# A fourth piece of w_in gets its low part on VectorE, and the written-out order and engine choices are replaced

## The chip, the cores and the metric

The kernel runs on one core of a Trainium2 chip. The metric is device time in microseconds (us). The core has five engines with queues of their own: TensorE (PE; PEld is its weight load), VectorE (DVE), ScalarE (ACT), GpSimd (POOL) and SyncE (SP), which only issues transfers here. Nearly all transfers are issued on SP's queue, in its order.

## The reference

Attention (4 batches, 8 heads, 576 tokens, 64 per head) with rotary tables, then a layer that multiplies by w_in (512 x 2048), applies a leaky function with a slope of its own per column, and multiplies by w_out; then a soft mixture of 8 experts with 4 slots each.

```python
x1, x2 = (x[..., :half], x[..., half:])            # rotate, for q and k
q_rot = concatenate([x1 * cos - x2 * sin, x1 * sin + x2 * cos])
attn = softmax(q_rot @ k_rot.T / sqrt(64));  x = (attn @ v) as 2304 x 512
h = x @ w_in
g = np.maximum(h, 0.0) + alpha * np.minimum(h, 0.0)
x = g @ w_out
logits = x @ phi                                   # 2304 x 32
d = softmax over tokens;  slot_input = d.T @ x     # 32 x 512
slot_out[e] = np.maximum(slot_input[e] @ w1[e], 0.0) @ w2[e]
out = softmax over slots of logits @ slot_out
```

## The kernel before

**Attention.** Heads go in pairs p = 0 to 3. Rotated keys and queries are made by `prep_qk` (loads, two multiplications by the tables, a sum; the first pair of batch 0 by `first_qk`, L341 and L346, in four parts so that the first scores come early). TensorE makes scores (L483 in batch 0; L492 to L496 in the later ones), VectorE their maximum (L501), ScalarE the exponential (L506), ScalarE or GpSimd the scaling (L228, L232). Batch 0 turns the probabilities on TensorE (L581, L631), copied out at L222 or L224; the other batches turn them in 32 x 32 blocks on VectorE (L568) and through DRAM. Products with the values are 20 matmuls (L665) for 256 tokens of a pair, or for the 64 that are left.

**First layer.** Tokens go in 9 blocks of 256. A chunk is 128 columns of w_in for one block: 12 matmuls of 128 x 256 in float16 (L842), 16 chunks to a block. Both operands are pairs of float16, a high part and a low part (what the high part leaves), and a chunk multiplies high by high, high by low and low by high. `logit` (L884) adds each group of four chunks to the block's logits. "Slots" of a block (`slots_late`, L1036) is a burst of 128 small matmuls, and stands eight times; the last block has another form (L1000).

**Weights.** w_in comes as 64-bit floats in 8 pieces j of 256 columns (`prep_w`, L704). For each: a load of 1 MB (L714), three VectorE instructions that build 32-bit floats (L736, L738, L740), the bound by ScalarE (L748), TensorE's spread of it over the partitions (L248) with a short VectorE chain, then the high part. The low part is made in one of two ways: for j below 5 by `split`, in two halves: a scaled diagonal (on one of three engines), TensorE multiplies it with the 32-bit weights (L288) and subtracts the high part (L289), and ScalarE or VectorE copies the result out. For j of 5 and more it is one VectorE instruction:

```python
nc.vector.scalar_tensor_tensor(dst(1), xv(), sw[:, j:j + 1], dst(0), ALU.mult, ALU.subtract)
```

The chunks of piece j wait for its low part (`w_ops[0, j]`). Pieces of w_out transposed come after, and give the weights of the logits (`wphi`).

**Order.** Every operation is listed in a Plan with its engine, what it depends on and the buffers it uses. Where an operation may go to one of several engines, `choose` takes the next digit of the string ENGINES. The string ORDER holds a permutation of all operations; they are issued in it, and each engine and queue works through its own ones in that sequence. `order` asserts that each stands behind what it needs. The costs and due times in the `op` calls take no part in the order that is run. In the tail, loads of w_out and of the expert weights (L1194, L1249) wait until attention's buffers are free, and some until the last block's slots are done.

Of the kernel before, what the change touches and what calls it, by code (L numbers as in the profile page):

```python
# [32 lines left out]


ENGINES = (
    "020000000201020000001001101011101110101010000110000100202000100200021000112000100110020010020000002011102020000200010001"
    "000000000020000200000202001000000000001202000200010000000000201010000100001002011000002202000000020120010000000000202000"
    "012211020020001000002020000000010000200220000021000000002000002002202200120220021000200202000202002200200220200021000202"
    "222000210110000000201020120000102220000002000201000201221000000200022000202001202200000220000000002200000000001102000021"
    "220000000000202000202000000201000220000000002200000202002000200001200000000200220000212010012010000201000000000000000100"  # L40
    "000101001001001010100001011100000011001001012010110000000000000110100100000100001111000000000000001000110100101100110001"
    "00010000000000101000101010000001000000011011001011000100000110011011010101"
)


ORDER = (
    "c-m!F2UrzH*WNRG@1<P23Mh(5FM<?B3?hjUeg%8^qsDw1#eywZ5aahL7-K=KNo+CZx1eZ5VnGnasDX%-"
    "2%<E_f=IDMka7{YyYtV??nQh)c<%1Z*>m3Wo^xjA%$<OIzB3>f0rD@vTQB7yq;44eM5BgrM|)0u@YwHeqhDu{|6|9;`au4It`2~Fe{e{5d8lvzha(X;23NeY0#mzU(<amG0A+<9Xu@ux"
    "e$VZ04H!g>93f?B-"
    "q3b^==})pdpW*d28WGj94_Crqt5J|A2erpJ5?6>I4Y`Nxb%EH7zzdu7uiFsN9>J)^T(p<&9Cm9x<K>D*4p@%jX6MNn{S@duEXxR<qsjvJUBe`zGvi9Yg6cY*Y9p%&C@ZjlZW>%^=&Wpc"  # L50
    ">CTXW_i2gl|jWra)ZhW7N;Y3^($u$#DxHaK-"
    "r7F&W+GRXi{}P^J(h!lD95t9Ch8%r7?2pJ0}qD1e@IkcerW!+F^GDn7B39^tH_ndaHtbGmZMi(XYdAyH<Ncs(Its%OXGA^r5+4rEO6UF!p<^e)X!w0p3HS(6<K(q|leIt1|-"
    "w%eI0s&{70;7KTu%{A2Du2!B3W^T@eKT^IbwD`Pa2fC)4NLeAA*&;DIuTkTRR4F8M2IyES2!yQu)&wUMEBzLL(4V<#xnOU!x3xR8<JC_cvICADrwQX<64ag11n+!!hQ203XTBu3Y`jy~"
    "xZDR7Azu-"
    "IZ8o-f=V_M~8<3HnWJR30o*W+#nKN(a2OWSXH+GKpHe_-)}5m%?BFE~6KQ~>JIv!Uj2e$x4vhc1IM;28)@_Gd%Kv_3zmj>DN5)@au%-_)d2uyV|mpOTYo4BJA{wiq+`*1Py-TE_7GYew"
    "hPPlpba{mu+h#wE{;-Vv0zf0N$HStnK7vo~zo0723G*iQ!9)Z;@d_QVC=T^D85*4U>lMU8TnkI3G;b)84)a%(VNe)<dd^36WV5NOz6J|%Bxh;O7_sDZ(m+wp7Bm4E{-"
    "k(zZEr#MucNB6wP?>;!oxPG%<`u`}dw62>zNIyJnTqh4M3E=>3cY`2x99+76HdoJZ!ll%f^=|$_Bes+tEQFCK`<&ipv3hFTNXT_AhuE@5>QM$0c|5n?IJ;r0GW&%)l)2Xg9jhwM-"
    "?QSu^@EYU@28$WGQg&X-"
    "%*=dwB`5v4;Gfzo{wL<#iZE;9hiYmn@k;hc6{Xc$#{Fi#h>4C;lQCaJ_Z)(#TV#w*yixJW@)DmnDZw?b3R#oz!dTA^#k4;&6qtxsog&_%Xh$$hz_s&`mPT_s0>Rtin{x-"
    "w&y=t|NDMl!Kab+R;Cp#Zt5E2)XAcH+v4`YWj`)9X@okrqMZ1uA{aaKKTjQuiXEDVpforRNE=t#&pXT34kA|WhGTQa9k*CfF~MMB<i4-^w1UylJn(+tivSizxbso9HsRy=M5oHU-"  # L60
    "G8L+Ub*K4%p+^|R>fEO!9S0C6r7fDCnHP*zrwWe1n?Z4Wb*8A{A24WLCyEhP1A>zjT?~v;q&)eGyC)zyJ=LwnWW6W5)C({0`#c>FrE@!Zv*Qg%gEQD<9LCw|HZ`Q%*oTd`5TK`UMl;a@"
# [103 lines left out]
def attn_moe_softmoe(ctx, tc, qx, kx, vx, w_in, w_out, alpha, phi, w1, w2, tab, msks, w_out_t, out):  # L165
# [538 lines left out]
    def prep_w(j, which, due):  # L704
        c = {}
# [53 lines left out]
        u = [s_raw, s_wx, s_w]  # L759
        o = run["raw"] = op(DMA, 2913, due + WD, load, [run["raw"]], takes=[s_raw], uses=[s_raw])  # L760
# [365 lines left out]
    n = 0  # L1126
# [21 lines left out]
    for b in range(B):  # L1148
        r = 64 * (b % 2)
# [33 lines left out]
    wo, s_wo, wo_op = {}, {}, {}  # L1183
# [39 lines left out]
    for base, half in [(b, h) for b in range(0, 24, 4) for h in range(2)] + [(b, h) for h in range(2) for b in (24, 28)]:  # L1223
        if True:
            for i in range(base, base + 4):
# [5 lines left out]
                n = 2 if key[:3] == (1, 1, 1) else 1  # L1231
# [443 lines left out]
```

## Time and profile before

| | us |
|---|---|
| median of 3 runs (564.83 to 568.68) | 564.88 |
| profiled execution | 566.71 |
| its span | 564.8 |
| TensorE busy in the span | 529.4 |
| VectorE busy | 478.4 |
| ScalarE busy | 335.7 |
| GpSimd busy | 269.5 |

The span is what the profile's times count from, and lies 1.9 us under the time of the execution that it was taken in. Busy time counts compute instructions only. A busy share is an average over stages with different limits, so the stages are read one at a time. In a table by stage a line gives the stretch, its length, then for PE, PEld, DVE, ACT and POOL in turn the busy us (and instructions), then the granted TensorE clock, the DMA share and GB/s. In a timeline the first two numbers are the start and the time from first start to last end of the instructions merged in that line.

### The profile page before, as it was taken

The numbers are of one execution on the slowest core, as the hardware profiler recorded it, in microseconds if no ns is written. First come the engines' busy times: TensorE is split into PE (matmuls) and PEld (weight loads), VectorE is DVE, ScalarE is ACT, GpSimd is POOL, SyncE is SP. The second block draws the span as 40 slices with busy tenths as digits, with TensorE's granted clock in tenths as the row PEclk, the third lists the DMA queues.
The fourth block names the chain that finished last, engine by engine and source line by source line (L and its number), as shares of the span: only waits on it lengthen the run. The fifth ranks groups of instructions, "written<-read, shape, count | busy, mean of one in ns | idle before, by whom it ended". The sixth has DMA issues, their size and how long they took to land.

```text
span 564.8 us, 14752 instructions
## 1 busy us (share of the span) xinstructions
PE 529.4 (94%) x5752; PEld 392.9 (70%) x5752; DVE 478.4 (85%) x1085; ACT 335.7 (59%) x817; POOL 269.5 (48%) x254
## 2 busy tenths in 40 slices
PE   3799999999999899999989899999999999999994
PEld 1455655778787587787867688877678877864464
DVE  4999999999999599999989599999866899865363
ACT  2999999898787377576677358576421222330220
POOL 3676854598879833678773478854110000001000
PEclk9999999999999899999999899999999999999998
DMA  8995758447999878698997778987864998899998
GB/s 296 395 339 181 233 172 243 136 145 264 291 327 332 272 234 298 199 344 296 324 288 231 260 233 279 335 283 247 268 230 166 412 408 332 324 379 381 404 366 238
DMA packets 80805, 160.74 MB, mean 285 GB/s; under 512 B 5344, under 2 KB 44640, under 8 KB 80736
## 3 DMA queue, kind: packets, MB, share of 16 engines
q1 hardware_dynamic: 80320, 159.45, 81.8%
q8 instruction: 45, 0.74, 0.5%
q10 hardware_dynamic: 416, 0.36, 0.3%
q14 instruction: 24, 0.20, 0.1%
HBM read 115.75 MB, written 36.96 MB: 270 GB/s over the span
## 4 chain that ended last, share of the span: by engine, by line
PE 73%; DVE 11%; ACT 6%; DMA 6%; issue 3%; SPq 1%; POOL 0%; DVEq 0%; ACTq 0%; POOLq 0%
PE ph L842 32%; PE pv L665 12%; PE st L496 8%; DMA xw<-in_moe_w_dram 4%; PE pu L1036 4%; PE lg L884 3%; DVE mm L501 2%; ACT e L506 2%; PE st L483 2%; DMA vt<-in_v_dram 1%; DVE w L740 1%; PE st L492 1%; DVE w L738 1%; PE pt L581 1%; PE st L494 1%
## 5 line engine op out<-in xcount | busy, mean ns | idle before, releaser
L842 PE MATMUL ph<-xt,w 128*128 128x256 f16 x1536 | 183.9, 273 | 2.1 <-issue 1.6
L842 PEld LDWEIGHTS <-w 128*128 128x128 f16 x1728 | 162.0, 98 | 31.8 <-issue 9.2
L506 ACT ACTIVATE e<-st,mm 128x576 f32<-128x576 f32 x144 | 106.2, 739 | 44.2 <-DVE mm L501 40.0
L501 DVE TENSOR_REDUCE mm<-st 128x1 f32<-128x576 f32 x144 | 105.3, 739 | 10.8 <-PE st L496 8.0
L232 POOL TENSOR_SCALAR e<-e,mm 128x576 f32<-128x576 f32 (+1 forms) x76 | 59.2, 785 | 86.6 <-DVE mm L532 56.1
L853 ACT ACTIVATE rl<-ph 128x256 f32<-128x256 f32 x110 | 41.1, 380 | 83.8 <-PE ph L842 79.6
L375 POOL TENSOR_TENSOR xn<-xn,tabs 128x576 f32<-128x576 f32 x52 | 78.7, 1522 | 25.4 <-DMA xn<-in_k_dram 12.5
L665 PE MATMUL pv<-ET,vt 128*64 128x256 f32 (+1 forms) x640 | 80.2, 397 | 1.1 <-ACT e L506 0.9
L568 DVE STREAM_TRANSPOSE tb<-e 128x512 f32<-128x512 f32 (+1 forms) x108 | 75.3, 705 | 0.5 <-ACT e L228 0.4
L496 PE MATMUL st<-ks,qs 128*128 128x288 f32 x384 | 74.3, 316 | 1.1 <-issue 0.9
L860 DVE SCALAR_TENSOR_TENSOR g<-rl,oma,ph 128x256 f32<-128x256 f32 x144 | 66.2, 465 | 9.6 <-ACT rl L853 8.6
L665 PEld LDWEIGHTS pv<-ET,vt 128*64 128x64 f32 (+1 forms) x640 | 44.5, 140 | 29.9 <-issue 6.0
L228 ACT ACTIVATE e<-e,mm 128x576 f32<-128x576 f32 (+1 forms) x78 | 56.6, 736 | 7.5 <-DVE mm L532 7.1
L496 PEld LDWEIGHTS st<-ks,qs 128*128 128x128 f32 x384 | 54.5, 189 | 5.7 <-issue 3.0
L876 DVE STREAM_TRANSPOSE gb<-g 128x512 f32<-128x512 f32 x64 | 43.7, 692 | 0.2
L483 PE MATMUL st<-ks 64*128 64x288 f32 (+1 forms) x168 | 30.2, 453 | 10.2 <-DVE ks L346 8.0
L378 POOL TENSOR_TENSOR xn<-xn 128x576 f32<-128x576 f32 x23 | 34.2, 1491 | 1.3
L400 POOL TENSOR_TENSOR qs<-xn,qs 64x576 fp32r<-64x576 f32 x21 | 30.8, 1466 | 7.9 <-ACT qs L222 4.7
L1056 POOL MEMSET edt<- 128x256 f32 x1 | 0.3, 312 | 68.5 <-DVE lp L1025 68.5
L483 PEld LDWEIGHTS st<-ks 64*128 64x128 f32 (+1 forms) x168 | 17.1, 191 | 20.2 <-POOL ks L346 7.4
L506 ACT ACTIVATION_READ_ACCUMULATOR e<-st,mm 128x1 f32 x144 | 28.4, 197 | 0.0
L228 ACT ACTIVATE xt<-pv,vb 128x256 f16<-128x256 f32 x26 | 12.2, 471 | 22.3 <-PE pv L665 19.7
(201 smaller groups left out, 820.7 us busy)
## 6 DMA issues: line engine op xcount, KB each, us to landing
sc<-tb SPq DMA_DIRECT2D x48, 576.0 KB, 4.2
ET<-sc SPq DMA_DIRECT2D x24, 1152.0 KB, 7.6
xw<-in_moe_w_dram SPq DMA_DIRECT2D x42, 512.0 KB, 9.0
xn<-in_k_dram SPq DMA_DIRECT2D x15, 576.0 KB, 6.4
xn<-in_q_dram SPq DMA_DIRECT2D x15, 576.0 KB, 5.6
wraw<-in_moe_w_in_dram SPq DMA_DIRECT2D x8, 1024.0 KB, 10.2
wraw<-in_w_out_t_dram SPq DMA_DIRECT2D x8, 1024.0 KB, 5.2
wor<-in_moe_w_out_dram SPq DMA_DIRECT2D x16, 512.0 KB, 10.1
```

The costliest lines, as they stand in the source:

```text
L228: nc.scalar.activation(dst, src, AF.Copy, scale=scale)
L232: nc.gpsimd.tensor_scalar(dst, src, scale, 1.0, ALU.mult, ALU.mult)
L375: engines[on].tensor_tensor(e["x"][:, w], e["x"][:, w], tabs[:, w], ALU.mult)
L483: nc.tensor.matmul(st[to, j, at:at + w], x, k[rows, z:z + w], start=True, stop=True)
L496: nc.tensor.matmul(st[:, j, 0:288], r["q"][:, 768 * h + 128 * s:768 * h + 128 * s + 128].bitcast(F32R), r["k"][:, a, h, ks].bitcast(F32R), ...
L501: nc.vector.tensor_reduce(c["mm"][:, h:h + 1], c["st", h][:, :, 0:288], axis=AX.XY, op=ALU.max, negate=True)
L506: nc.scalar.activation(c["e"][:, h].rearrange("p (a n) -> p a n", a=2), c["st", h][:, :, 0:288], AF.Exp, bias=c["mm"][:, h:h + 1], accum_o ...
L568: nc.vector.transpose(out=to if tail else to[:, :, 0:8].rearrange("p q (m h) j -> p q m h j", h=2)[:, :, :, h], in_=e.rearrange("p (m q j) ...
L665: nc.tensor.matmul(pv[r], v[k, 4 * h + i if i < 4 else 8 + (h if b else 0)], x, start=(i == 0), stop=(i == 4))
L842: nc.tensor.matmul(ph, wi[j][:, wp, kc, 128 * fo:128 * fo + 128], xt[:, xp, kc, :], start=(n == 0), stop=(n == 3 * KC - 1),)
L860: nc.vector.scalar_tensor_tensor(blk["g", j][:, fo, :], c["r"], oma[:, f:f + 1], c["ph"], ALU.mult, ALU.add)
L876: nc.vector.transpose(out=blk["gt", j // 2][:, f % 8 - 1:f % 8 + 1, :].rearrange("p c n -> p (c n)"), in_=blk["g", j][:, fo - 1:fo + 1, :] ...
```

## The change

Piece j = 4 takes the VectorE way of the low part. ENGINES is a new string with 791 digits (before 794, three choices of `split` are gone), and ORDER is a new permutation of 2787 operations (before 2791: one diagonal, two pairs of matmuls and two copies fewer, one low part more). No other line of the program is changed.

```diff
 ENGINES = (
-    "020000000201020000001001101011101110101010000110000100202000100200021000112000100110020010020000002011102020000200010001"
...
+    "000000000200020000000111000101010101000000000100000202010000001020200110001010011000200000000112020000020001200000110002"
...
 ORDER = (
-    "c-m!F2UrzH*WNRG@1<P23Mh(5FM<?B3?hjUeg%8^qsDw1#eywZ5aahL7-K=KNo+CZx1eZ5VnGnasDX%-"
...
+    "c-m!F4M0q3_rK@fX_{uHloBOL2@w^EQmKSWRuqL|*GJ2;*6Q7SW+PM<i@#msUA?|uRQgo0NMw9Qs--U<QHc<lYMN&5-2Z)^d#A?#KQ(vmbDnd4=XcKYJm)-"
...
         o = scaled = op(on, 1040, due + WS, hi, [o], uses=[s_wx, s_w])
-        if j >= 5:
+        if j >= 4:
             w_ops[0, j] = op(DVE, 1130, due + WS, lo, [scaled], uses=[s_wx, s_w])
             return
         dg = [None]
```

The strings can be decoded and compared. Of the 791 choices that both kernels have, 282 name another engine. All choices of an operation over the whole run, before and after:

| operation | before | after |
|---|---|---|
| high parts of w_in | 7 ScalarE, 1 VectorE | 8 ScalarE |
| copies of `split` | 9 ScalarE, 1 VectorE | 8 ScalarE |
| first keys and queries, multiplications | 3 VectorE, 1 GpSimd | 4 VectorE |
| first keys and queries, sums | 2 VectorE, 2 GpSimd | 4 VectorE |
| other rotations (two a load) | 8 VectorE, 52 GpSimd | 12 VectorE, 48 GpSimd |
| copies of turned probabilities | 32 ScalarE, 4 VectorE | 36 ScalarE |
| scaled outputs of attention | 38 ScalarE, 10 VectorE | 31 ScalarE, 17 VectorE |
| evacuations of the final output | 7 ScalarE, 12 VectorE | 11 ScalarE, 8 VectorE |

In the order, SP's first load is now piece 0 of w_in (before the first keys), and VectorE converts that piece ahead of all operations on the first keys and queries. TensorE's order has the same operations ahead of batch 3's last product, in a somewhat changed sequence; ahead of the burst of `slots_late` of block 2, one product stands where there were two, and ahead of that of block 5, three.

## Rows read from the trace of the kernel before

**Rows 1.** The page: busy time of engines, then the chain that ended last, by engine.

```profile
PE 529.4 (94%) x5752; PEld 392.9 (70%) x5752; DVE 478.4 (85%) x1085; ACT 335.7 (59%) x817; POOL 269.5 (48%) x254
...
PE 73%; DVE 11%; ACT 6%; DMA 6%; issue 3%; SPq 1%; POOL 0%; DVEq 0%; ACTq 0%; POOLq 0%
```

**Rows 2.** Busy time by stage, whole span.

```profile
0.00:118.30 118.30, 101.52 (x720) 62.65 (x720) 108.48 (x209) 101.92 (x238) 72.71 (x62) 1.00 0.72 246
118.30:420.00 301.70, 293.42 (x3328) 232.75 (x3327) 271.82 (x635) 202.72 (x501) 194.26 (x188) 0.99 0.83 275
420.00:510.00 90.00, 89.08 (x1045) 69.95 (x1047) 73.80 (x165) 22.02 (x60) 0.72 (x3) 1.00 0.87 331
510.00:564.80 54.80, 45.38 (x672) 27.54 (x664) 24.33 (x79) 9.01 (x19) 1.84 (x2) 0.95 0.97 347
```

**Rows 3.** Timeline of TensorE at the tail; waits of the sync queue: total, times, longest.

```profile
506.27 1.92 PE L1000 MATMUL pu<-gt,dn 128*32 128x512 f32 x16 [0.19 <-DVE dn L994]
...
SPq L1249 <- PE pu L1000: 3.6, 1, 3.6
```

**Rows 4.** Busy time by stage, stretches inside the prologue.

```profile
0.00:115.84 115.84, 99.06 (x699) 61.39 (x700) 106.06 (x201) 99.46 (x233) 70.49 (x59) 1.00 0.74 250
7.47:30.00 22.53, 17.26 (x74) 10.09 (x75) 19.68 (x39) 16.61 (x38) 13.72 (x11) 1.00 1.04 393
30.00:60.00 30.00, 29.24 (x193) 17.14 (x192) 29.86 (x69) 29.78 (x70) 21.81 (x14) 1.00 0.72 246
```

**Rows 5.** Waits of TensorE, 118.3 to 420 us: us in total, times, longest.

```profile
PE pv L665 <- issue: 2.4, 1, 2.4
...
PE pu L1036 <- issue: 1.6, 1, 1.6
...
PE st L496 <- issue: 0.9, 1, 0.9
```

**Rows 6.** Timeline of TensorE (start, us); instructions of L756 (ns min/median/max).

```profile
49.65 1.10 PE L288 MATMUL rest<-wx,dg 128*128 128x512 f32 x2
...
50.80 1.02 PE L288 MATMUL rest<-wx,dg 128*128 128x512 f32 x2
...
L756 DVE SCALAR_TENSOR_TENSOR w<-w,sw x1: 1269/1269/1269, 107.0 to 107.0; 128x1024 f16<-128x1024 f32 x1
```

**Rows 7.** VectorE's groups by shape, 0 to 118.3 us: count, busy us, mean ns.

```profile
L375 DVE TENSOR_TENSOR xn<-xn,tabs 128x576 f32<-128x576 f32 x8 | 6.1, 767 | 0.1
...
L224 DVE COPY ET<-pt 128x512 f32<-128x512 f32 x4 | 2.7, 673 | 0.0
...
L230 DVE TENSOR_SCALAR xt<-pv,vb 128x256 f16<-128x256 f32 x2 | 0.9, 467 | 0.0
```

**Rows 8.** Timeline of the start, all engines: start us, us, operation, idle before and releaser.

```profile
0.74 0.70 SPq L338 DMA_DIRECT2D xn<-in_k_dram  x1
...
4.89 0.76 DVE L341 TENSOR_TENSOR xn<-xn,tabs 128x576 f32<-128x576 f32 x1 [4.02 <-DMA xn<-in_k_dram]
...
7.47 1.33 PE L483 MATMUL st<-ks 64*128 64x288 f32 x4 [7.47 <-DVE ks L346]
...
12.06 0.78 DVE L736 TENSOR_SCALAR w<-wraw 128x1024 int32<-128x1024 int32 x1
...
12.48 2.92 PE L483 MATMUL st<-ks 64*128 64x288 f32 x8 [1.80 <-ACT e L506]
...
14.13 1.22 DVE L740 SCALAR_TENSOR_TENSOR w<-wraw,w 128x1024 int32<-128x1024 int32 x1
```

**Rows 9.** Busy time by stage: after two stalls, then a stalling and a clean burst.

```profile
190.60:194.60 4.00, 4.00 (x22) 2.58 (x21) 1.69 (x4) 0.00 (x0) 3.92 (x4) 0.57 0.97 278
316.00:320.00 4.00, 4.00 (x41) 2.10 (x23) 2.84 (x6) 0.00 (x0) 0.41 (x1) 0.66 1.07 318
289.10:291.80 2.70, 2.70 (x134) 1.82 (x136) 2.48 (x6) 2.67 (x7) 0.60 (x2) 1.00 0.95 302
485.10:487.80 2.70, 2.70 (x132) 1.82 (x136) 2.70 (x7) 0.68 (x2) 0.00 (x0) 1.00 0.90 308
```

More of the change, by code (lines that the diff above doesn't have):

```diff
@@ new lines @@
+    "200200000101000002222000202000200200220000000000002002000000000202000200010020000201200000200000212000001200121000202000"
+    "000000000202200000201021010200202000200012200000000221120000200210000002110000200000020100000002022000200001212001020221"
+    "000000102202001202000000201000020121000102000000202002010010201021100000200202000200010002201220021100000000000000100000"
+    "000000110000000010000201110010000000100002000001100110000001120010010000000000000000001010001100010012001100010100000000"
@@ L43 @@
+    "02000000110100100101100000000110011010000011010000101101000111000111101"
 )
 ORDER = (
[L47 to L50 removed]
@@ L51 @@
[L51 to L61, printed above, removed]
@@ new lines @@
+    "O!Xipdi*`G6Dn?b)w^Yq`7;=QqijpB67SY4mfj`P6$@t!f@6V`8+`7%!!56(7t3WCbItldjWZb5I-"
+    "Qrm#E0Gnk1dVfg4n#Py3Xy>vp&<HZ0tKI_LV$?<^ZOwZb7MwBr}xF+S?LW5p#uPrfZ%Bbe06XsSE%pl^glyns}F(-L+3$movv<?>y_OkyqtQQil)t%RXeC<<9GEDq)Ds6E@CiHM5a{C-"
+    "ZT~a>q}$i2;q_B?_@u*sMk8=AZPHnRF}5Rt}Qa9$)$*ZDS2Y7|MoxPKq#2iIBo)7<(zu0*()F3WpP*T6QcfWYMY9eZDC^7G`-"
+    "!Fr<FP<<VxT$InPQji6trBxS|nS@8MB%BoA^ykJtOTGt!|1r|pCy7uqz$S*O6el&#SZ%@w*m!uZV5ABFt-o9ko^2&sC3-"
+    "9K0A4zMY%IQu_pRI14UbmpqEx6eNnj=@hT$k%6=@l_X@hd>QZ`>o-s;t}478vZ9EY!=mIa4m)wIx2L!vcOy-t0V2(KIY`j9m+3l#mua*89MrqY-27(+4-"
@@ new lines @@
+    "%Lf{{p6<+tpRKhN~d;L!vk^$(0?OP5kGo~})_8z_N?0I2nKTo^Y?jBq;{g)(RVW;HwjzYK%Pckn1UH36qwA`Ca@R^wG<$p~cR5q@}J7EaOj&_8_=FfF6@;w0~Mr97G8$JQ#aBr%A)&;2"
+    "s99sIDGeVKo$0LhQjZVHZX8kntB|AIjWDPw80TuE4<n4RlGQbZ>Y2g()k!vf*E$icMd#x%OO5Qw!%^%=yd}euPc&j<_(z;<t_C#a%CFI=0--"
+    "%4slj2TZ0N0B*XD#2;0g@Fdoincea6u_$=)Wh6oGTokLVNyP$I-"
+    "`6E;{nyx4<lefdHcmAJ1$6^Y@lU$GjZAP*6`!C0|#|b0eqyP4?e=Le>{vPnVfG07S1Aez0hpQ~_IaXGc?iZco^tX`Kq>L)Va;;>7e9JK`$MK2jEmyEbohiRvGD@TaDTpLdiw8AZ3IK0h"
+    "pmaXD+UeiywrFPZFjjl7X`sabM1d*irAiPwLJh34epMa54CM3Q^0mY?#s`~o%E5S0^qmI5ycrSSkZ(-"
@@ new lines @@
+    "oq$@N?T}&;BkDZR!=e;Tx~gvFmn5Hx~bUAa&vVUsCUQ8anIAQBT*$O>8i1KfN}vXg8!hIR8WFW6+eE!XK*>gP`O`fnQ0#_+Xpe8<JyxYrH8FNPh47lu~cB%Eo|+Z#|UQqJi;so!<prIu"
+    "1Wt)!g`g)uqWsBO$s0Ce0>4$5zD3Jfpf`$=K-q@&T*kVAp|l8xnFMlpa%?Hp^*SSp3HPG=N3-w$S>&&8-"
+    "fw*%w!x@jSL&A7EM6qiV9y{|X5~K<n8B?!V<L=#2A}L%GE3;PCCYeQtOP^lm$mGQ-"
+    "BxXVMpvkYhQm?dqQkEfoG>v>JS;{^V&IQUC=><v(wmL}|?b01I$ToAAIP<eE=%R<bqN0WElLQ#^R~{DJT-WV*K-S~#cA+7^E~L%#J*P&!DuY6DbnuX^2Fc-"
+    "YwgLeYhmA7mAlZ%RVkV9WN*&}_Rd=Zg<L1Izb^ugHT>(3c@c-D3JZ9nxv?8O$^qgZNDu!TZ-Zb+y<OfQ5p}{!StOHL=YQ5<^D8=lUUzm#v?hwx(@6Gv%oAzrkA<Ua86pwttp=Z0I4C)0"
@@ new lines @@
+    "S;Vl7^l95+JS}B(Ab~F0g^zfu8AMv3siEgV&1pnH|y&vie9!j?es#+<`k5TMJ&L3WYz59WoX_85eX}^KffAB|38G>Cv&{OTFG3cKq|p{!KRkZaj?1Gxi4etx|7~<N*7df#sJrY@g~;@M"
+    "v85%?I%J^b<KNP6_)smzP9YCKdoBvAyNq7LU{=+kf3&G!-"
+    "Vh%oqqOH%x_?Im_A>B<VxHWxkQHR2B&T^$RLi?1xIHLZM%=(sno`yc+;<)NaM;8T<0{4GzUY!s@;IQkqsK{T|1R4{1)>zdYxb?+pE&U4<<xz|d-"
+    "TcGYIcgs2uN%s(j<BoCf$Y}O=F8YKNBj+${x9#tB<W#?H4SJS!SD*C|2O-"
+    "y>kPR&&~6tV8`wA_W?Q=Sp4eDp#Ev|#!Ym?cW9Oj&Ti;(%dLny<*1QpuH;xtf_9Y%PPjBxVQ0OFbYbtV5b1pQq?n<gGfgCS%dTf+ce^(!&|&JJhR97p4@=&Q6RZSC6cM%WDsSJhT-"
@@ new lines @@
+    "iWnErdYvxX6IzZvNYURn_Vm-*)i}Yq*tO9uUOW2PmR_7SDLCyTZIes})AlT-Ds|^^G=go@Wa^<SgguqLIs+!S@BdkA}<#-$FeefK4%oy_4-"
+    "+@M_;bkH{^(WItvFXtJjdoBs42;y(!TBQu&@7%CIv=Rnh49Ye-"
+    "3Ld_;QJCF!4Rx84R_~}IY6C^nhEpvl#R8gu1tB5uy@$1J(36Y_gsgLhdZMU+hbtw#nGehyLLdPD>aO|2NG*3`5(bBW7UHR0{G-"
+    "n`NcEU(e0`F?I3WFw2DBiC^YU9TK#l)_?$<y8yK}{t_PQnFLjW1R_)q+c~fW>^KgWbeiyr$j2`rF@jT<!lE1|M%#)cO0J0ZDVRSh~vdt6(0IF`OfEGTtwtfq?Q1%=I{Ac8A7+BY*|0{z"
+    "b#ABBtYdsB+lm_m4AS<d{AXErdH~eJYde3Yf_s+@I^Ciq$i^4Un-"
+    "7+_u4}J4O$QFxifY63I@3RZkkmdt}X@Ki~Cl)l5FYI1TDtD>tr=Q=nmSh?R3+Sw|ipP;;`*~rc9t&Gs@y)2?&d#(zNGYE<lBr8OC1kh$ovd(`2OM6te;2$>-"
@@ new lines @@
+    "fyh*PXGGeC)M#CE+H4Sho8bV74Bk(XBFP#Xqyb0|L3kE!G<eWe*c;cKrmLspo22Ejg#DjOrP7_E4eQ|O$>=!X3H4F{}t1^6wa1>kuks?nN=_3x<n&55NFO88{C>jW)#6^e`gaNo9Nt#7"
+    "rA+em}fEXi;9w;;>80<isTnzy{zuw&7^dj;MiP>>0iM(r-"
+    "Fe<OcA_$b&5k;s7fr=FhRY*^u!v4{NWEBN?lKmnTWK5Gd9QF;#Sa(8hir)%Y5y=ULCK+T%P^?HmAaH?_L@($Kj|nuVrj(RM$B^HdlnQGR0*)R#gESBqhV#b_urktN1ZtiHfei&pp^`)^"
+    "%tgR3gmx#g5hHyp!t2KKp$Q=;W_p7_n~GAB95IB-sC!Ntj!VVzWJ6F>1df>{L1@^AKuz?7fQQ&8!JPzxqA8ZFfMB$Wm=8s0u_*@WQfgkELGWsZ4;KxY-gDJ+;E_6kaM=g?<2L|<QcPeO"
+    "A2TZ=2sMA2I4Q*-"
@@ new lines @@
+    "8i<S*h3Gl)6#G<T5ek?G;&j+h2{c5AYKq;;0?spb!0M2k8&XZMTS1L}ks@bJ@f0Y6PbtYB8SDki8T5k<)SOEcCQF46gB#H3C{P>)7Kc!CxZ2vrXAV2Uq|v)JHP}DzjGIPGw8c=H8O}GQ"
+    "rHU7t=KN!JC=C?eHEj3<Dl!a7v)QC*?nqD!&2W?0A>zz%&d`7zkzBMS&1m^zhcr?rQG6tgY6LD=7?C6pBnQMTA*;r!Adduk!CB`j6~X()i^;MAG(v!^0DHvh$N^%Yl^`gz8U*&waQf_1"
+    "t*z{A3P=XKL&gNAj<k>smra7RB(ws)qmXEqa4xVFiG$!s=<r}@Egh_Y_c)&*wnE|xgs0FycG}aPSW~v_(%i`)+2!Q=0*L~`K{323c8i51s#GW&Xw2ZSSreRcoFtqmj7@8s6rs%(Du*~w"
+    "1dAwZI0WE#6(*>=z69@=;R>`Cj}u@%m=T{FY{-^#TuM<-;xM@U5Cq-"
```

45 lines of the change are left out of this document (10 added, 35 removed).

## The prediction

> **What bounds the kernel now.** I read the page first. TensorE is busy 94% of the span, VectorE 85%, and the chain that ended last is 73% TensorE, 11% VectorE [rows 1]. So an edit counts only if it shortens TensorE's own work or its idle time, and only where TensorE ends last. The table by stage says where that is [rows 2]. Batch 0's attention and the preparation of the weights (0 to 118.3 us) leave TensorE 16.8 us idle (118.3 - 101.5). The middle (to 420) leaves it 8.3 idle of 301.7, the next 90 us 0.9, and the last stage 9.4, at a DMA share of 0.97. The waits of the tail show why the last stage is different: the sync queue's weight load waits 3.6 us for TensorE's "slots" of the last block, which run from 506.27 for 1.92 us [rows 3], so until about 508 us TensorE sets the pace and a microsecond saved there moves all that follows; after it the transfers do, and the change leaves their bytes alone.
>
> The first stage has two near-bounds. Between 30 and 60 us VectorE is busy 29.86 us and TensorE 29.24 [rows 4]. TensorE's first matmul, on the first keys and queries, starts at 7.47 [rows 8]. In the middle the largest waits are "issue", in which TensorE waits for no engine and no transfer [rows 5].
>
> **Part 1: piece 4's low part goes from TensorE to VectorE.** Removed on TensorE: two halves of a piece. The timeline has the halves starting at 49.65 and 50.80, so 1.15 us each [rows 6]: -2.3 us. Removed beside it: two copies out of PSUM and one scaled diagonal, on engines whose own queues hide them. Added: one VectorE instruction at 1.27 us [rows 6]. Before, one of the ten copies was VectorE's; after, none is. Behind the new instruction stands whatever VectorE has next, and the chunks' matmuls on piece 4 wait for it; those come after the prologue, far behind.
>
> **Part 2: the engines chosen anew.** Decoding both strings, 282 of 791 choices differ. What matters is VectorE ahead of the last product (probabilities by values) of batch 0, which starts at 115.84 us; VectorE is busy 106.06 us until then and TensorE 99.06 [rows 4]. Onto VectorE come: the low part, +1.27; three of the eight operations on the first keys and queries that GpSimd did (a VectorE neighbour takes 0.76 [rows 8]; one is 4/3 as wide, two have a third to two thirds of its elements), about +2.0; three rotations at 0.77, +2.3; two sums over the same 576 columns, costed as rotations, +1.5; four scalings of attention outputs at 0.47, +1.9 [rows 7]. Off it go four copies of turned probabilities at 0.67, -2.7 [rows 7], and the one split copy that VectorE made, as large, -0.7. Six more (three off it: a high part and two small copies; three onto it) net to about -1.0, an estimate from rows of like size. Sum +4.6, so 110.7 us of VectorE work. ScalarE, busy 29.78 of the same 30 us [rows 4], is close too, but by the same count about 1.4 us of its work ahead of that product goes away, so I don't let it set the end.
>
> **Part 3: the start.** The sync queue now issues the 1 MB of weight piece 0 ahead of the first keys; before it stood behind five other loads of that queue. The first load, 288 KB, was issued at 0.74 and used at 4.89 [rows 8], 4.15 us later. Piece 0 has 736 KB more; at the 393 GB/s of 7.5 to 30 us [rows 4] that is 1.9 us, so it lands near 6.8. Then VectorE converts it (12.06 to 15.35 before, 3.3 us [rows 8]) to about 10.1, while keys, queries and tables arrive, and only then does the first keys and queries: 2.2 us more, first scores at about 12.3 instead of 7.47 [rows 8]. What was late first is early now: the conversion ended at 15.35 before, so ScalarE's bound and TensorE's maximum over partitions can come some 5 us sooner.
>
> Now the two bounds on the end of the stage. **By TensorE**: 99.06 - 2.3 = 96.8 of work, 12.3 of empty start, and the later waits. Those are 16.8 of idle, less the first 7.47 and an early gap of 1.80 [rows 8], so 7.5; half kept gives 112.9, that is -3.0 against 115.84. **By VectorE**: 110.7 of work, plus an empty start of at least 6.8 less the 0.9 of small work it can do meanwhile: 116.6 at least, +0.8; with 2 us of waiting on the first scores (TensorE itself stood 1.80 there before) it is +2.8. The nearest rows, VectorE at 99.5% from 30 to 60 us against TensorE's 97.5% [rows 4], lie between, since neither engine's order is rigid around that mark. I take **-0.6**, the middle of -3.0 and +1.8 (VectorE's two values), and keep -3.0 and +2.8 for the range. So I think three quarters of the 2.3 us is given back.
>
> **Part 4: the middle.** TensorE has the same matmuls ahead of the last attention product, by the decoded orders: 104 chunk multiplications, 30 logits, six slots. What can change is its idle time. Semaphore instructions stand on its queue, but products that have one among their 20 matmuls take as long as those without, so I cost those whose signal is already there at nothing; a late one shows as a wait, and of the 8.3 us idle there all but 1.8 is the issue stalls. If that cover goes (ScalarE or VectorE late by 2 us at several products), it costs those microseconds in full.
>
> The "issue" stalls are the larger term. They follow eight bursts of 128 small matmuls (slots, L1036): after the burst at 184.7 TensorE stands 2.4 us [rows 5], works at a granted clock of 0.57 in the next 4 us (partly 1.2 GHz in place of 2.4), so 1.7 us more [rows 9]; the other three are 1.6 (two of them, one row shown) and 0.9 [rows 5], and one of those has a slow stretch too, at 0.66 [rows 9]. Four of the eight bursts stall, all four with the DMA engines at least 0.95 busy in the burst; the four that don't have at most 0.90 (that nearest pair stands in [rows 9]). Together 6.5 us of standing and 3.4 of slow clock: near 10 us, 2.5 a stall. The stalls fit a queue of instructions that runs dry when small matmuls come faster than busy DMA engines deliver them. In the new order the bursts have the same 128 matmuls with other neighbours: before one there is now one product where there were two, before another three. At a middle DMA share of 0.83 [rows 2] I expect three or four stalls, **-1.2** (3.5 instead of 4), between none (-10) and all eight (+10). The Trainium skill, Runtime: NRT & Kernel Launch, "Instruction fetch mechanics", says that instructions are fetched in blocks of 256 over the sequencer's own DMA queue and that this is mostly hidden. One burst is 256 instructions (128 weight loads, 128 matmuls), which agrees; hidden it isn't here if the 2.4 us are such a fetch. By its "hidden" they are not, and rival D below holds.
>
> **Part 5: the tail.** Block 7's slots and a turn of the last block now stand later among the last chunks, the expert outputs change places among themselves, and some copies move from VectorE to ScalarE, which is busy 22 and 9 us in the last two stages [rows 2]. The bytes behind the last gate are the same. Zero, between -2 and +2.
>
> **Sum.** -0.6 - 1.2 + 0 = -1.8. The profiled execution took 566.71 us (span 564.8), so it would be 564.9; the median of the runs, 564.88, lies 1.83 under the profiled one: **about 563**.
>
> **Rivals.** *A, the stalls go (0.20).* If the new places of the bursts meet idle DMA engines, none or one stall is left: -6.3 to -8.8 on top, 554 to 557. For: four bursts passed clean. Against: the transfers around them are as many. *B, VectorE starves the prologue (0.20), the slower side.* Place: batch 0's last product. The condition: VectorE idle more than 5.1 us (115.84 - 110.7) before it, and my estimate is at least 5.9. Then the 2.3 us is on no path, and the part does not do what it says. With 9.9 us idle (6.8 at the start and 3.1 on scores at half clock) the mark comes 4.8 later, in place of 0.6 sooner: 568.5. Against: its orders put work behind that mark too, and TensorE has score rows to do in the gap. *C, more stalls (0.10).* Six to eight bursts: +6 to +11, 569 to 574. *D, the stalls belong to something that the order leaves alone (0.06)*: the same four stay, 0 in place of -1.2, 564.3. For: TensorE's matmuls are the same; against: their split at DMA share 0.90 to 0.95. My forecast (0.44) is 560 to 567 alone.
>
> **The numbers.** A measurement of this kernel can tell about 1% from no change, so faster means under 559.2 and slower above 570.5. Faster: A and a little of the forecast's edge, 0.21. Slower: most of C and little of B, 0.09. Same: 0.70. The range leaves out half of A and most of C: 556.5 to 569.5.
>
> **What would show it.** First scores at 11 to 13 us; split instructions 16 instead of 20 and four of L756; TensorE's busy time in all about 2.3 lower; VectorE busy over 110 us ahead of the last product of batch 0, which starts between 112.6 and 118.6; three or four "issue" stalls of over 0.9 us near the bursts. I am wrong if that product starts outside, if the number of stalls is under two or over five, or if the last block's slots end at another distance from the end than 56 us.

## The result and the profile after

The changed kernel takes 558.5 us (median of 4 runs, 557.74 to 560.26), the kernel before 565.05 on the same chip: a ratio of 0.987 (95% interval 0.983 to 0.991). Run again on another chip beside other kernels it was 557.83 against 563.57, 0.990 (0.988 to 0.993). So it is about 1% faster, 6.5 us on the first chip. Its profiled execution took 560.26 us with a span of 558.4, 6.4 below the span before.

The page of the changed kernel, busy time and the chain that ended last; the lines are those of [rows 1]:

```profile
PE 526.2 (94%) x5746; PEld 392.8 (70%) x5746; DVE 477.0 (85%) x1086; ACT 335.5 (60%) x814; POOL 262.3 (47%) x254
...
PE 67%; DVE 13%; DMA 7%; POOL 5%; ACT 4%; issue 2%; DVEq 0%; POOLq 0%; ACTq 0%
```

Counted on TensorE, the 6.4 us are 3.2 us less busy (529.4 to 526.2) and 3.2 us less idle (35.4 to 32.2 of the span). The table by stage says where the idle time went; columns as in [rows 2]:

```profile
0.00:118.30 118.30, 101.78 (x739) 64.30 (x740) 110.80 (x214) 103.12 (x240) 62.42 (x54) 1.00 0.73 246
118.30:420.00 301.70, 297.20 (x3381) 237.13 (x3379) 275.45 (x644) 200.86 (x498) 196.30 (x194) 0.99 0.85 281
420.00:510.00 90.00, 88.86 (x1068) 66.40 (x1069) 72.17 (x168) 21.43 (x57) 2.62 (x5) 1.00 0.89 343
510.00:558.40 48.40, 38.32 (x572) 24.93 (x564) 18.53 (x62) 10.14 (x20) 0.95 (x1) 0.90 0.94 332
```

The first stage is as idle as before (16.5 us), the middle went from 8.3 to 4.5, and the last stages rose from 10.3 to 11.2. The waits of TensorE from 110 to 420 us (total, times, longest), against [rows 5], show what left the middle:

```profile
PE pv L666 <- DMA ett<-sc: 1.8, 1, 1.8
PE lg L885 <- DVE g L861: 0.8, 1, 0.8
PE st L497 <- issue: 0.8, 1, 0.8
PE st L497 <- ACT e L507: 0.5, 2, 0.3
PE pu L1037 <- issue: 0.5, 1, 0.5
```

Two stalls on "issue" of 1.3 us in all stand where there were four of 6.5 us. Two waits that were not there before, on a transfer and on VectorE, took part of the room. The start, from the timeline, answers to [rows 8]:

```profile
0.74 0.45 SPq L715 DMA_DIRECT2D wraw<-in_moe_w_in_dram  x1
...
6.48 0.69 DVE L737 TENSOR_SCALAR w<-wraw 128x1024 int32<-128x1024 int32 x1 [4.42 <-DMA wraw<-in_moe_w_in_dram]
...
11.52 2.49 PE L484 MATMUL st<-ks 64*128 64x288 f32 x8 [11.52 <-DVE ks L347]
```

To follow the gain along the program I took from each trace when the same work ends: the last multiplication of the first block (chunk 16), of the last block (chunk 144), and the span's end. All kernels of this study, in us; "stalls" counts the waits on "issue" above 0.4 us between 118 and 500 us and their sum:

| kernel | first scores | chunk 16 | chunk 144 | between | end | stalls | median, ratio to before on the same chip |
|---|---|---|---|---|---|---|---|
| before | 7.47 | 153.3 | 500.7 | 347.4 | 564.8 | 4, 6.5 | 565.05 |
| changed | 11.52 | 150.1 | 492.0 | 341.9 | 558.4 | 2, 1.3 | 558.5, 0.987 |
| changed, again | 11.59 | 151.6 | 491.8 | 340.2 | 558.0 | 2, 2.1 | 557.83, 0.990 |
| before + 64 matmuls | 8.36 | 155.0 | 502.1 | 347.1 | 565.1 | 4, 6.6 | 565.96, 1.004 |
| before + 32 matmuls | 7.55 | 153.9 | 488.0 | 334.1 | 553.4 | 0 | 556.4, 0.987 |
| before + 32, again | 7.35 | 155.0 | 491.1 | 336.0 | 557.3 | 0 | 556.17, 0.987 |
| changed + 48 | 11.48 | 152.7 | 500.4 | 347.7 | 566.5 | 2, 4.8 | 563.38, 0.999 |
| changed + 24 | 11.99 | 150.5 | 490.6 | 340.1 | 558.3 | 2, 2.5 | 558.98, 0.993 |
| before, low part alone | 7.41 | 160.4 | 502.7 | 342.3 | 566.8 | 4, 6.2 | 568.94, 1.008 |
| before, start alone | 11.82 | 158.2 | 501.9 | 343.7 | 566.0 | 4, 6.8 | 571.43, 1.012 |
| changed, low part undone | 11.39 | 154.3 | 495.7 | 341.4 | 562.1 | 1, 1.9 | 564.02, 1.001 |
| changed, start undone | 7.16 | 151.9 | 493.2 | 341.3 | 559.7 | 1, 2.4 | 560.41, 0.995 |
| joint at 700 | 11.62 | 154.4 | 489.1 | 334.8 | 552.8 | 0 | 556.36, 0.987 |
| joint at 900 | 11.48 | 151.1 | 490.1 | 339.0 | 556.2 | 0 | 556.48, 0.984 |

Between before and changed, 3.2 us come in the prologue (1.7 in the second profile), 5.5 between the two marks, and 2.3 are lost behind the last chunk (64.1 us to 66.4). Each row is one profile, and two profiles of one kernel differ by up to 1.5 us at chunk 16, 3.1 at chunk 144 and 3.9 at the end, so a smaller difference in a column tells nothing by itself.

### The profile page after: what moved, and what is told of

Read it like the earlier page. It is cut to its first block, busy times and chain, and to the rows that moved or that the text cites. A ratio compares the mean times of both kernels' runs of the same rounds, so it can differ in the third digit from the quotient of the medians.

```text
span 558.4 us, 14714 instructions
## 1 busy us (share of the span) xinstructions
PE 526.2 (94%) x5746; PEld 392.8 (70%) x5746; DVE 477.0 (85%) x1086; ACT 335.5 (60%) x814; POOL 262.3 (47%) x254
## 4 chain that ended last, share of the span: by engine, by line
PE 67%; DVE 13%; DMA 7%; POOL 5%; ACT 4%; issue 2%; DVEq 0%; POOLq 0%; ACTq 0%
PE ph L843 28%; PE pv L666 11%; PE st L497 7%; PE lg L885 3%; DVE mm L502 3%; PE pu L1037 3%; PE ph L1369 3%; DMA xw<-in_moe_w_dram 2%; DMA sc<-tb 2%; PE st L484 2%; PE pt L582 1%; ACT e L507 1%; POOL xn L376 1%; PE po L1430 1%; DMA ett<-sc 1%
## 5 line engine op out<-in xcount | busy, mean ns | idle before, releaser
L233 POOL TENSOR_SCALAR e<-e,mm 128x576 f32<-128x576 f32 (+1 forms) x79 | 65.1, 829 | 80.6 <-DVE mm L533 60.3
L376 POOL TENSOR_TENSOR xn<-xn,tabs 128x576 f32<-128x576 f32 x48 | 69.5, 1456 | 22.3 <-DMA xn<-in_k_dram 19.6
L666 PE MATMUL pv<-ET,vt 128*64 128x256 f32 (+1 forms) x640 | 76.9, 385 | 0.0
L666 PEld LDWEIGHTS pv<-ET,vt 128*64 128x64 f32 (+1 forms) x640 | 42.5, 136 | 28.1 <-issue 7.9
L401 POOL TENSOR_TENSOR qs<-xn,qs 64x576 fp32r<-64x576 f32 x22 | 32.1, 1460 | 18.2 <-ACT qs L223 17.0
L379 POOL TENSOR_TENSOR xn<-xn 128x576 f32<-128x576 f32 x22 | 32.8, 1491 | 1.3
L484 PEld LDWEIGHTS st<-ks 64*128 64x128 f32 (+1 forms) x168 | 16.5, 185 | 20.9 <-DVE ks L347 12.2
L582 PE MATMUL pt<-idf,e 128*128 128x128 f32 x144 | 21.7, 284 | 1.9 <-ACT ET L223 1.3
L885 PE MATMUL lg<-g,wph 128*32 128x256 f32 x288 | 22.4, 389 | 0.8 <-DVE g L861 0.8
```

The lines of the kernel that those rows point to most:

```text
L233: nc.gpsimd.tensor_scalar(dst, src, scale, 1.0, ALU.mult, ALU.mult)
L376: engines[on].tensor_tensor(e["x"][:, w], e["x"][:, w], tabs[:, w], ALU.mult)
L484: nc.tensor.matmul(st[to, j, at:at + w], x, k[rows, z:z + w], start=True, stop=True)
L666: nc.tensor.matmul(pv[r], v[k, 4 * h + i if i < 4 else 8 + (h if b else 0)], x, start=(i == 0), stop=(i == 4))
```

## What stalls TensorE: a count

The four stalls of the kernel before look different on the timeline: one stands among short products, one among chunks, one inside a burst, one among scores. Here is the first, on TensorE's timeline of the kernel before, and then the DMA queues from 188 to 190.6 us (packets, MB, share):

```profile
186.93 0.54 PE L1036 MATMUL pu<-gb,lp 32*32 32x256 f32 x11
187.40 0.80 PE L665 MATMUL pv<-ett,vt 128*64 128x64 f32 x18
190.57 0.27 PE L665 MATMUL pv<-ett,vt 128*64 128x64 f32 x2 [2.38 <-issue]
```

```profile
q1 hardware_dynamic: 290, 0.66, 96.6%
q8 instruction: 1, 0.02, 2.3%
```

The stall breaks a run of 20 like matmuls after the 18th, and the profile shows nothing that it waits for; in this stretch one packet moves on the instruction queue q8 (188.09 to 189.04). I counted TensorE's instructions ahead of each stall in the trace's records: two for a matmul record (its weight load and itself) and one for each semaphore instruction.

```
kernel    stall at  matmuls  semaphores  instructions
before    188.19    1470     67          3007 = 11*256 + 191
before    293.15    2602     108         5312 = 20*256 + 192
before    313.80    2853     118         5824 = 22*256 + 192
before    398.37    3733     150         7616 = 29*256 + 192
changed   292.10    2607     98          5312 = 20*256 + 192
changed   311.19    2858     107         5823 = 22*256 + 191
changed   183.99    1446     60          2952 = 11*256 + 136   (waits for a transfer)
changed   225.52    1908     72          3888 = 15*256 + 48    (waits for VectorE)
```

All waits on "issue" stand at one residue (191, or 192 beside it), the two waits with an owner do not. In the fourteen profiles of the table there are 26 such stalls above 0.4 us between 118 and 500 us, and 26 stand at 191 or 192. The instruction queue carries 45 packets of 16 KB over the run of the kernel before, 64 bytes for each of 256 instructions. So the sequence is fetched in blocks of 256, and a stall is the end of a block that was used up before the next had come. In the kernel before, the blocks that ended in a stall held 3.2 to 4.7 us of work (most blocks hold 12 to 15), and work and stall together made 5.5 to 6.3. The Trainium skill, Advanced Engine Details and Errata, "ISA Cache", gives lines of 256 instructions; the count agrees.

The times of these packets say more. Number the block ends and the packets of a run from its start: packet k goes with block end k. In all 26 stalls TensorE goes on 1.2 to 1.6 us after the end of its packet, whatever the stall's length. Of the other 455 block ends between 118 and 500 us, all but one come 1.2 us or more after theirs (the one, 1.0 us after, stalls for 0.37 us). So a short block alone is no stall: its packet must also be late. The kernel before has seven blocks under 5.6 us of work there, four that stall and then three that pass:

```profile
184.97:188.19 3.22, 3.22 (x146) 2.27 (x115) 1.59 (x6) 2.35 (x4) 1.04 (x1) 1.00 1.04 398
289.15:293.15 4.00, 4.00 (x142) 2.38 (x142) 3.76 (x10) 3.95 (x9) 1.90 (x3) 1.00 0.97 297
309.11:313.80 4.69, 4.69 (x131) 3.16 (x127) 3.32 (x10) 4.37 (x12) 2.46 (x3) 1.00 1.03 348
393.77:398.37 4.60, 4.60 (x149) 2.98 (x117) 4.60 (x14) 1.55 (x4) 0.98 (x2) 1.00 1.04 347
411.93:415.67 3.74, 3.74 (x130) 2.52 (x136) 3.72 (x11) 2.01 (x7) 1.07 (x2) 1.00 0.95 331
465.05:469.00 3.95, 3.95 (x144) 2.56 (x144) 3.92 (x9) 0.39 (x1) 0.00 (x0) 1.00 0.48 167
482.99:487.10 4.11, 4.11 (x129) 3.25 (x134) 4.08 (x10) 1.47 (x3) 0.72 (x3) 1.00 0.73 244
```

In the four the packet starts 3.0 to 4.0 us into the block, in the three 1.5 us into it at the latest. The last but one column is the DMA share: 0.97 to 1.04 in the four, 0.95, 0.48 and 0.73 in the three. In all fourteen profiles 23 of 24 such blocks that stall have a share of 0.97 or more, and 4 of 30 that pass. So busy DMA engines go with late packets, with exceptions on both sides; no run changes the share alone, so that they cause the delay is not shown.

## The experiments

**Moving the block ends.** Theory 1 (a stall is the end of a block that comes too soon) was tried by putting matmuls that count for nothing ahead of TensorE's first work; engines and order stay.

```diff
                 for g in heads if 0 in js else ():
                     c["st", g] = ps_s.tile([128, 2, 512], F32, tag="st", name="st")
+                if js == (0,):
+                    for _ in range(64):   # 64, 48, 32, 24
+                        nc.tensor.matmul(c["st", 0][0:32, 0, 0:16], idf[0:32, 0:32], idf[0:32, 0:16], start=True, stop=True)
```

> The kernel before with 64 small matmuls (128 TensorE instructions, 32x32 by 16 columns on the identity, overwritten by the first scores) put ahead of TensorE's first work, where it stands idle until 7.47 us. Order and engines unchanged. Theory 1 (blocks): TensorE's stalls stand where the count of its instructions, semaphores included, is 191 or 192 modulo 256, 4 of 4 before and 2 of 2 after, so they are the ends of 256-instruction blocks, and a stall is about 5.6 us less the work that the block holds. Counted on the trace of before, moving the ends by 128 instructions leaves one block that holds only 2.7 us (at 227 us, where the DMA engines are half idle) and one of 5.4, where there were seven under 5.6: the four stalls at 188, 293, 314 and 398 us go, the slow clock behind them too, one may come near 230. 556 to 560 us. Theory 2 (my prediction's): the stalls go by the DMA share while the burst runs, which nothing here changes: the same four stalls, 564 to 566. Theory 3 (the neighbours of a burst in the order): unchanged too, 564 to 566.

Measured: 565.96 us, 1.004 (1.001 to 1.007), four stalls of 6.6 us in the same places. A miss, until the trace was counted: each of these 32-bit matmuls is two matmul records, so 64 are 256 instructions, one whole block, and the residue of every later instruction is what it was. It became the control: the matmuls themselves cost 1 to 2 us and move nothing.

> The changed kernel with 48 such matmuls (96 instructions) ahead of TensorE's first work, idle until 11.52 us. Theory 1 (blocks): the ends move by 96 instructions; counted on the trace of after, blocks under 5.6 us become five (2.7 at 179, 4.7 at 284, 4.2 at 385, 3.2 at 454, 3.1 at 484 us) in place of four that hold 5.0 or more, 8.6 us more in all if each stalls as long as it may; with the slow clock behind long stalls 563 to 568 us, and stalls of 1 us and more near 182 and 454 to 490 us that were not there. Theories 2 and 3: 557 to 560, like the changed kernel.

Measured: 563.38 us, 0.999 (0.996 to 1.002). By the same count the shift was 192 and not 96. Its two "issue" stalls, 3.05 us at 314 and 1.76 at 417, stand at 191 and 192, in the blocks that a shift of 192 makes short, and the ones at 292 and 311 are gone. Right in kind, wrong in place, by my count of the edit.

> The kernel before with 32 small 32-bit matmuls ahead of TensorE's first work. The trace of the run with 64 of them shows that each is two matmul records and so four instructions: that run moved the block ends by 256, a whole block, and was a control, with the four stalls where they were. These 32 move them by 128. Theory 1 (blocks of 256 instructions): the four stalls at 188, 293, 314 and 398 us go; one block that holds 2.7 us of work is left at 227, with the DMA engines half idle, so a stall of 0 to 2.5 near 230; 5 to 9 us less than the control from 180 to 400 us, the end at 557 to 561 in the profile. Theory 2 (DMA share in the burst) and theory 3 (neighbours): the same four stalls, the end within 2 us of the control.

Measured: 556.4 us, 0.987 (0.984 to 0.990). All four stalls are gone; the end came at 553.4, 11.6 us before the control's, and a second set of runs gave 556.17, 0.987 (0.984 to 0.991). The waits of TensorE from 118 to 496 us in this kernel, of 6.5 us on "issue" before:

```profile
PE st L499 <- issue: 0.2, 1, 0.2
```

And the bursts at 184.4, 283.6 and 304.5 us, table by stage:

```profile
184.40:187.10 2.70, 2.70 (x132) 1.82 (x130) 0.88 (x3) 2.49 (x4) 0.18 (x2) 1.00 1.04 400
...
283.60:286.40 2.80, 2.80 (x134) 1.89 (x136) 2.56 (x8) 2.77 (x7) 0.72 (x2) 1.00 1.01 295
304.50:307.30 2.80, 2.80 (x134) 1.93 (x132) 0.75 (x4) 1.95 (x5) 0.81 (x1) 1.00 1.05 419
```

The DMA share is 1.04, 1.01 and 1.05 in bursts that stalled before, with the same neighbours, and none stalls now. So theories 2 and 3 fail as they stand: neither the share of the burst nor its neighbours make a stall where no short block ends. An edit that adds work and changes no order is worth as much as the whole change.

> The changed kernel with 24 such matmuls, 96 instructions. Theory 1: stalls at instruction counts of 191 or 192 modulo 256, near 182 (up to 2.9), 389 (up to 1.4), 457 (up to 2.4) and 487 us (up to 2.5); the ones at 292 and 311 go or stay under 1 us; 563 to 568 us in the profile. By the run with 48 of them (192 instructions: stalls at 314 and 417 us, where the count on the trace of after had the blocks of 3.3 and 2.7 us) I lean to theory 1. Theories 2 and 3: the stalls of the changed kernel, 558 to 560.

Measured: 558.98 us, 0.993 (0.990 to 0.995), 558.3 in the profile. Stalls came at 182.5 (1.81 us) and 454.9 (0.73), both at 192, and none at 389 or 487, though the blocks there held 4.2 and 3.1 us. So the residue says where a stall can be, not that there is one. Likewise the block of 2.7 us at 224 in the kernel with 32 matmuls passed. What lets a short block pass is its packet, which in these three starts between 1.1 us before the block and 0.3 us before it; what sets the packet's start (where the fetch stood in the queue, or the traffic of that moment) stays open, and the size that I had counted, 8.6 us, was an upper end.

> The kernel before with the 32 matmuls again, beside the hybrid on one chip: 0.984 to 0.990 of the kernel before, no stall at 191 or 192 modulo 256.

Measured as expected, 0.987, no such stall.

**The low part alone, and undone.**

```diff
-        if j >= 5:
+        if j >= 4:
...
 # ORDER: piece 4's diagonal, matmuls and first copy taken out,
 # VectorE's instruction where its last copy stood; ENGINES: its three digits taken out
```

> The kernel before with one part of the change alone: piece 4's low part by one VectorE instruction at the place of its last copy, all other operations in the old order on the old engines. If TensorE ends the prologue: 2.3 us less there, block 16's last chunk about 2.3 us earlier; the ends of blocks move by some 13 instructions in later stages, which by count changes the stalls by less than 1 us: 562 to 563. If VectorE ends it (my rival B): nothing gained, 564.5 to 566.

Measured: 568.94 us, 1.008 (1.005 to 1.011). Both branches missed: chunk 16 ends 7.1 us later than before. In the old order, at the place of the last copy, the part is worse than nothing. The waits of TensorE from 45 to 62 us:

```profile
PE pv L653 <- DVE mws L239: 2.0, 1, 2.0
PE pc L619 <- DVE mws L239: 1.1, 1, 1.1
PE top L236 <- ACT w L736: 1.1, 1, 1.1
```

The first two wait for VectorE's reduction of a weight piece's maximum (L239 in this kernel), which VectorE reaches late. By stage, from 45 to 60 us (TensorE's waits) and from 60.1 to 66.9:

```profile
45.00:60.00 15.00, 10.12 (x61) 5.49 (x57) 15.00 (x20) 11.35 (x24) 10.42 (x6) 1.00 0.45 141
60.10:66.90 6.80, 6.36 (x41) 4.19 (x43) 4.81 (x17) 4.76 (x11) 3.83 (x3) 0.50 0.82 284
```

VectorE is busy all of the first stretch and TensorE idle for 4.9 us of it; in the second the granted clock is 0.50 (1.2 in place of 2.4 GHz), which is up to 3.4 us of TensorE's time. The kernel before has neither there. Five of the 7.1 us come back up to chunk 144; there this kernel has as many stalls but a granted clock of 1.00, where the kernel before loses 3.4 us to the slow clock.

> The changed kernel with piece 4's low part given back to TensorE (the diagonal and both copies on ScalarE) at the place in the order where VectorE's instruction stands, all else as changed. If TensorE's 2.3 us are on the path in the new order: chunk 16 ends 2 to 4 us later, 561 to 563. If the gain of the prologue comes from the order alone: the same as changed, 558 to 560. Block ends move by some 13 instructions after 65 us, which by count adds 1 to 2 us of stalls.

Measured: 564.02 us against 557.83 for the changed kernel on the same chip, ratios of 1.001 (0.998 to 1.004) and 0.990. Against the second profile of the changed kernel chunk 1 ends 2.6 us later and chunk 16 2.7 (4.2 against the first), and TensorE is busy 2.2 us more until chunk 1 ends (96.3 to 94.1): in the new order TensorE's 2.3 us are on the path in full. One stall, 1.94 us at 293 with 1.7 us of slow clock behind it, stands where the changed kernel has two of 2.1 in all.

**The start alone, and undone.**

```diff
 # ORDER: the load of piece 0 moved to the front, its three conversions ahead of the
 # first multiplication of the first keys (undone: the load behind the first keys, queries
 # and tables; conversions, bound and spread behind the first scores)
```

> The kernel before with only the start of the change: the load of weight piece 0 first on the sync queue, and its three conversions ahead of the first keys and queries on VectorE. Engines and the rest of the order as before (so GpSimd still does three of the eight operations). If the early piece is what helped: the first scores come 4 us later but chunk 16 ends 1 to 3 us earlier, 562 to 564. If the late first scores cost what they seem to: 566 to 569, and the rest of the order had to make up for it. My prediction's bounds for this part alone: -1 to +3.

Measured: 571.43 us, 1.012 (1.008 to 1.016): more than the worse branch. Chunk 16 ends 4.9 us later, also outside the bounds of -1 to +3.

> The changed kernel with the old start: the load of piece 0 behind the first keys, queries and tables, its conversions, bound and spread behind the first two scores' maxima and exponentials. First scores near 8 us instead of 11.5. If the early piece is needed by the new order: chunk 16 ends 1 to 5 us later, 559 to 563. If the early piece only costs 4 us of empty TensorE, as it did when it was put alone into the old order (5 us later): 2 to 4 us earlier, 554 to 556. The count of instructions ahead of the bursts stays within a few, so the stalls stay.

Measured: 560.41 us, 0.995 (0.992 to 0.998). First scores at 7.16, and yet chunk 16 ends 0.3 us later than in the second profile of the changed kernel and 1.8 later than in the first. TensorE waits later for what now comes later, the bound of the first piece:

```profile
PE top L236 <- ACT w L736: 6.9, 1, 6.9
```

The second branch is out. The time lies in the first branch's range, but a shift of 0.3 to 1.8 us is no more than two profiles of one kernel differ: in the new order no run shows that it matters for the prologue which of the two comes first.

> The changed kernel itself again, beside the following ones on one chip: 0.983 to 0.991 of the kernel before, as on its first run.

Measured: 0.990 (0.988 to 0.993).

**Both gains together.**

```diff
 # ORDER: the changed order's first 700 (900) operations, then the rest as before
 # ENGINES: by the same division; 36 matmuls ahead of the first scores
```

> The first 700 operations of the changed order (to about 140 us: the prologue, with piece 4 on VectorE) with their engines, then all others in the order and on the engines of the kernel before, and 36 small 32-bit matmuls ahead of TensorE's first work (it stands idle until 11.5 us there), so that the block ends of the middle lie as in the kernel before with 32 of them. If the two gains are apart from one another (2 to 3 us less in the prologue from the new order, the stalls gone from the old middle): chunk 16 ends at 150 to 152 us, the middle takes 334 to 336 us from there to the last chunk, 550 to 553 in the profile, 2 to 3 us below the kernel before with the 32 matmuls. If the new prologue's gain is bound to its own middle: no better than that one, 553 to 556.

Measured: 556.36 us, 0.987 (0.983 to 0.990); no better than before + 32. The first blocks came early (chunk 8 at 129.7), chunk 16 did not.

> As the hybrid, but with the first 900 operations in the changed order (to about 165 us, behind the last chunk of the first block), since the earlier joint at 700 gave the prologue's gain away: chunk 8 ended 3.2 us earlier than in the kernel before with 32 matmuls, chunk 16 only as early as there, with two waits of 0.7 us behind the joint. If the joint was the loss: chunk 16 ends at 150 to 152 us and the middle takes 334 to 336 from there, 550 to 552 in the profile, 0.980 to 0.985 of the kernel before, the fastest of all. If the new order's prologue leaves its work to the middle instead of saving it: chunk 16 early, the middle longer by as much, 0.985 to 0.990 again.

Measured: 556.48 us, 0.984 (0.981 to 0.987). Chunk 16 comes at 151.1, 3 to 4 us earlier than with the old prologue, and the middle takes 339.0 in place of 334 to 336: the second branch. TensorE waits for VectorE and ScalarE there:

```profile
PE lgt L934 <- DVE g L851: 1.1, 1, 1.1
PE ph L833 <- ACT lt L210: 0.7, 1, 0.7
```

All three kernels without stalls stand at 556.2 to 556.5 us, 1.3 to 1.6% under the kernel before on their chips. Their intervals overlap with one another's and with the changed kernel's (0.987 and 0.990), so which of the four is fastest the runs can't tell.

## Why the prediction was right or wrong

The time fell in the range, past the forecast's own end of 560 and short of rival A, and under 559.2, which the prediction called faster and gave 0.21. The direction was right, and both large steps were mis-sized: the last product of batch 0 came 2.6 us sooner (1.1 in the second profile) for 0.6, and the middle gained 5.5 us for 1.2. That the range held is partly luck: the tail lost 2.3 us that no term had, and without them the time would have been 556.2, outside it. Of the signs named, the first scores came as said; TensorE's busy time fell by 3.2 us for 2.3, VectorE was not busy over 110 us ahead of that product, the stalls were two (none over 0.9 us in the first profile) for three or four, and the last block's slots end 58.7 us from the end, for 56.6 before, which the prediction named as a sign of being wrong.

**Part 4, the stalls: half of the reason.** The step said that the stalls fit a queue of instructions that runs dry, and then that the DMA share in the burst decides, from eight bursts that it divided without a miss. The changed kernel has bursts at shares of 1.02 and 0.97 without a stall (453.7 and 483.8 us), and the kernel with 32 matmuls at 1.04 and more. Which bursts can stall is decided by where the multiples of 256 fall, semaphore instructions included; the share divides only the short blocks among them, and not without a miss in the other kernels. I costed semaphore instructions at nothing because a satisfied one costs no time; in the count they weigh as much as a matmul. The rows for it were there: one position modulo 256 for four stalls. The term was -1.2 us; idle time of the middle gives -3.8 (8.3 to 4.5), and the slow clock from 152 to 500 us, by the granted clock in stretches of 4 us, falls from 3.4 us to 1.7 (0 in the second profile), and the 1.7 stand behind the wait for a transfer at 184, not behind a stall. Counted over all shifts of the new order's trace, in steps of 16, the position it stands at leaves blocks the least short of 5.6 us: 1.5 us in all, against about 11 for the old order where it stood. Moving the changed kernel's block ends by 192 took its whole gain away (0.999), though the matmuls that moved them are themselves 1 to 2 us of that. Rival D, with the stalls left as they are, is out. The Trainium skill, Runtime: NRT & Kernel Launch, "Instruction fetch mechanics", calls the cost of such a fetch mostly hidden: most of the 45 are, and the late ones of short blocks are not.

**Parts 1 and 2, VectorE's load.** "Three quarters of the 2.3 us is given back" failed: undoing the part costs all of it. The step that failed is VectorE's 110.7 us ahead of the last product of batch 0. That product starts at 113.22 (114.73 in the second profile), inside the bracket that I gave and near its bound by TensorE (112.9), and VectorE was busy 105.7 us by then, no more than before:

```profile
0.00:113.22 113.22, 96.70 (x696) 60.63 (x696) 105.72 (x206) 98.44 (x230) 58.68 (x51) 1.00 0.76 256
```

The operations came as decoded. But among the conversions, whose longest took 2.31 us before, none is long now. The third instruction of a conversion in the kernel before (count, then min/median/max ns over the whole run), and in the changed one up to 118.3 us:

```profile
L740 DVE SCALAR_TENSOR_TENSOR w<-wraw,w x12: 1199/1224/2306, 14.1 to 127.3; 128x1024 int32<-128x1024 int32 x12
```

```profile
L741 DVE SCALAR_TENSOR_TENSOR w<-wraw,w x11: 1199/1225/1241, 8.5 to 102.8; 128x1024 int32<-128x1024 int32 x11
```

Over all conversions ahead of that product that is 3.2 us (51.1 to 47.9 by groups); another 1.1 is a conversion that has hardly begun when the product starts. I had taken busy time as work. What made the conversions long before isn't settled. That the low part alone costs 7.1 us, with TensorE waiting for a VectorE that is busy without a pause, shows that rival B's mechanism is real in the old order; the new order is what keeps it away, and I had no way to price that from the two counts.

**Part 3, the start.** Piece 0 in use at 6.48 (6.8 forecast), first scores at 11.52 (12.3): the step was right. Its weight was not: undone in the new order it moves chunk 16 by 0.3 to 1.8 us, and TensorE's empty time only moves.

**Part 5, the tail.** Zero, within 2 us, was forecast; it lost 2.3. From the last chunk to the end the kernels with the old tail take 63.0 to 66.3 us, those with the new one 66.2 to 67.7: the new tail is likely the longer by one or two, but the two ranges touch and no run isolates it.

**What stays open.** The joints show that the prologue's 3 us and the stalls' gain don't add: with a clean middle the early prologue only made TensorE wait later. For the changed kernel as a whole, then, the fewer stalls are shown to be worth what it gained (before + 32 has as much, and changed + 48 has nothing left), and the low part is shown to be needed in its order; that it adds to the end in a middle without stalls is not shown.

## What to carry to other kernels

When an engine stands on "issue" in the midst of like instructions, count its instructions from the start, semaphores included, before looking at neighbours or at the DMA load: one residue at all such stalls names the fetch of blocks, and the instruction queue's packets say which of them come late. A fixed number of cheap instructions at an idle place then moves every block end at once, and a whole block of them is the control. An order that is searched with busy times alone doesn't see this, and an experiment that adds or removes instructions moves the ends too, so each needs its stalls read before its time is.

## What was not expected of the hardware

A 32-bit matmul is two matmul records and counts for four instructions (64 issued, 128 in the trace). TensorE's bursts use up 256 instructions in 2.75 us. Where it stalled in the kernel before, the short block's work and the stall take 5.5 to 6.3 us together, but 4.1 to 7.4 over all fourteen profiles: what is steady is the 1.2 to 1.6 us from the packet's end to the next matmul. Behind two of the four stalls, of 2.38 and 1.65 us, the granted clock fell to 0.57 and 0.66 over 4 us in the kernel before [rows 9]; stalls of 2.3 and 2.5 us in the kernel with the start alone left it at 1.00. From 152 to 500 us it was 1.00 throughout in the kernel with 32 matmuls, which gains by that as well.
